# A gated-mix kernel on one core: the down projection of its feed-forward as 2x2 block products in Strassen's form, with GpSimd making sums of blocks

## The chip, the core and the metric

The kernel runs on one core of a Trainium2 chip. The metric is the device time of one execution in microseconds (us). The core's engines are named as the profile names them: PE (TensorE, matmuls), PEld (its weight loads), DVE (VectorE), ACT (ScalarE), POOL (GpSimd) and SP (SyncE, which issues the DMAs). Before the change the median of three runs is 1704.81 us (1704.14 to 1707.67).

## The reference

```python
x = A_x                                             # 1 x 2048 x 576, float32
g = sigmoid((x * gate_w).sum(-1, keepdims=True))    # one gate per token
qkv = x @ wqkv                                      # 32 heads of 18
phi = lambda p: concat([softmax(p), softmax(-p)])   # of q and k after w_phi, per head
kv, z = sum_s phi_k v, sum_s phi_k                  # linear attention
a = (phi_q kv / (phi_q z + 1e-6)) @ wo
gate, up = x @ W_gate, x @ W_up                     # 576 x 4608 each, on the same x = A_x
b = (gate * (gate > 0) * up) @ W_down               # 4608 x 576
out = g * a + (1 - g) * b
```

Every product is float32 by way of two fp32r parts (high and low) of each operand, so that a float32 product is three matmuls: high x high, high x low, low x high.

## The kernel before, in words

The program has two stages. The first (0 to some 415 us) is the attention: projections of 16 tiles of 128 tokens, softmax features, `kv`, and, in four blocks of 512 tokens, the quotient (`sums`, `invert`, `divide`) and the output projection (`project_out`), whose rows go to a DRAM tile `att`. They are scaled by g on the way. POOL works only here (`scale`, L182: one of the two softmax halves of each tile).

The second stage, the feed-forward, runs from some 417 us to the end. Tokens stand along the free dimension. Its outer loop has two halves `hf` of 1024 tokens (two blocks t of 512), its inner loop 36 chunks `c` of 128 hidden rows: 72 units `u`. Gate and up of a chunk, for both token blocks, are a 2x2 block product in Strassen's form (Winograd's variant): seven products `product(ps, u, n, first)` (L720) of seven matmuls of 128x512 each. Their token operands `XO[hf, n]` (tiles `xo`) are made once for each half by `x_operands`: sums of blocks of x on DVE, then high part on ACT, low part on DVE. Their weight operands `wb` and `ws` are made for each chunk from one 768 KB load `wr`: `split_blocks` takes the high and low parts of three blocks (ACT L604, DVE L607, and 32 rows of a third low part, L608), `split_sums` makes four sums of blocks on DVE (L621 to L624, in place) and takes the parts of these. The products accumulate in the PSUM tiles `cx`, `ca`, `cy`; ACT copies three stages of them out (L789, L794, L800), DVE adds the others (L805, L810, L815) and ends with two `scalar_tensor_tensor` that form relu(gate) x up for the two blocks (L822). `split` (L123, L124) takes high and low of each, `hh` and `hl`.

The down projection is a plain product. After every two chunks `down(hf, g)` (L763) adds up the 576 output rows in ten pieces: five row blocks m (four of 128, and one that holds the last 64 rows, high and low) for two token blocks t. A piece takes 6 matmuls, or 4 for the last block: 8 x 6 + 2 x 4 = 56 for two chunks. Two pieces stay in PSUM (`pm`) through the half, eight go through `pd` and are added by DVE to SBUF accumulators `ac` (L770). Its weights come by a load `wdr` and `split_down` (ACT L708, DVE L709, L710). After the last group `finish` multiplies each piece by 1 - g (`ngb`, L740), adds the row block `ga` loaded from `att` (L741) and stores it.

Each engine runs its queue in order. In the feed-forward the order is that in which the tile framework's scheduler puts the instructions of the code; `in_order` pins the code's order on DVE, ACT and SP for the few instructions that `later` traces. The generator `down` is stepped between products, so that the pieces of the group before stand among the products of the present chunks.

## Time and profile before

| what | value |
|---|---|
| median of three runs | 1704.81 us |
| the profiled execution: its time, and its span from the first to the last instruction | 1707.41 us, 1705.6 us |
| PE busy in the span | 97% (7834 matmuls) |
| DVE, ACT, POOL busy in the span | 76%, 37%, 3% |
| mean granted clock of PE | 0.98 |
| bytes read from HBM, written | 108.50 MB, 16.74 MB |

The span is cut into groups by line: a group's row has its instructions' count, the sum of their busy time, the mean of one in ns, and the idle time of the engine just ahead of them with what ended it. Matmuls overlap, so that the 390 ns of one 128x512 matmul is not what it costs; that is read from a stretch in which PE never waits. The window view gives, for stretches of the span, each engine's busy time and count, the clock and the DMA share.

### The profile page before, as it was taken

The numbers are of one execution on the slowest core, as the hardware profiler recorded it, in microseconds if no ns is written. First come the engines' busy times: TensorE is split into PE (matmuls) and PEld (weight loads), VectorE is DVE, ScalarE is ACT, GpSimd is POOL, SyncE is SP. The second block draws the span as 40 slices with busy tenths as digits, with TensorE's granted clock in tenths as the row PEclk, the third lists the DMA queues.
The fourth block names the chain that finished last, engine by engine and source line by source line (L and its number), as shares of the span: only waits on it lengthen the run. The fifth ranks groups of instructions, "written<-read, shape, count | busy, mean of one in ns | idle before, by whom it ended". The sixth has DMA issues, their size and how long they took to land.

```text
span 1705.6 us, 19899 instructions
## 1 busy us (share of the span) xinstructions
PE 1648.6 (97%) x7834; PEld 1379.0 (81%) x7834; DVE 1291.1 (76%) x1966; ACT 624.0 (37%) x895; POOL 46.0 (3%) x53
## 2 busy tenths in 40 slices
PE   9999997988999999999999998999999999999996
PEld 8899995666888888888888886788888888888885
DVE  5877675666778777777778779977777777777776
ACT  4233335554533333333323334433333332333330
POOL 0121210000000000000000000000000000000000
PEclk9899997889999999999999999999999999999998
DMA  5211113535221211122122212421111222121203
GB/s 182 69 37 58 44 44 96 170 127 169 83 70 65 70 51 60 61 65 70 51 70 66 70 51 70 149 83 62 63 61 52 70 65 70 51 70 60 63 18 105
DMA packets 42329, 128.48 MB, mean 75 GB/s; under 512 B 4906, under 2 KB 5546, under 8 KB 42236
## 3 DMA queue, kind: packets, MB, share of 16 engines
q1 hardware_dynamic: 42236, 127.22, 23.1%
q8 instruction: 61, 1.00, 0.2%
q14 instruction: 32, 0.26, 0.0%
HBM read 108.50 MB, written 16.74 MB: 73 GB/s over the span
## 4 chain that ended last, share of the span: by engine, by line
PE 86%; DVE 5%; DMA 4%; ACT 2%; issue 1%; SPq 1%; DVEq 0%; ACTq 0%
PE cx L720 26%; PE pd L763 19%; PE ca L720 13%; PE cy L720 6%; PE pm L763 5%; PE pq L150 4%; PE pk L150 3%; PE pv L150 3%; PE kv L319 2%; PE pwo L150 2%; PE ptr L283 1%; DMA ga<-att 1%; PE po L150 1%; DMA xr<-xs 1%; DMA wdr<-wd 1%
## 5 line engine op out<-in xcount | busy, mean ns | idle before, releaser
L763 PE MATMUL pd<-hh,wd 128*128 128x512 f32 x1008 | 357.5, 390 | 2.2 <-DVE ac L770 2.2
L720 PE MATMUL cx<-xo,ws 128*128 128x512 f32 x1008 | 253.2, 390 | 5.3 <-DVE ws L608 2.2
L720 PE MATMUL cx<-xo,wb 128*128 128x512 f32 x1008 | 252.5, 390 | 2.8 <-DVE o L556 1.4
L720 PE MATMUL ca<-xo,ws 128*128 128x512 f32 x1008 | 253.4, 390 | 0.8 <-DVE ws L608 0.6
L720 PEld LDWEIGHTS cx<-xo,ws 128*128 128x128 f32 x1008 | 188.8, 188 | 46.6 <-ACT g L789 2.7
L763 PE MATMUL pd<-hl,wd 128*128 128x512 f32 x576 | 224.6, 390 | 0.0
L720 PEld LDWEIGHTS cx<-xo,wb 128*128 128x128 f32 x1008 | 188.9, 188 | 43.8 <-DVE o L556 1.9
L763 PEld LDWEIGHTS pd<-hh,wd 128*128 128x128 f32 x1008 | 189.4, 188 | 43.1 <-DVE ac L770 3.5
L720 PEld LDWEIGHTS ca<-xo,ws 128*128 128x128 f32 x1008 | 189.2, 188 | 42.2 <-ACT wd L708 1.0
L770 DVE TENSOR_TENSOR ac<-pd,ac 128x512 f32<-128x512 f32 x272 | 187.5, 690 | 33.1 <-PE pd L763 33.1
L123 ACT ACTIVATE hh<-g 128x512 fp32r<-128x512 f32 x144 | 83.0, 621 | 294.3 <-DVE g L822 294.3
L708 ACT ACTIVATE wd<-wdr 128x576 fp32r<-128x576 f32 x72 | 48.8, 679 | 262.2 <-PE pd L763 256.0
L604 ACT ACTIVATE ws<-wr 128x1536 fp32r<-128x1536 f32 x72 | 107.3, 1490 | 59.5 <-DVE wr L624 59.5
L720 PE MATMUL cy<-xo,wb 128*128 128x512 f32 x504 | 126.6, 389 | 0.0
L763 PEld LDWEIGHTS pd<-hl,wd 128*128 128x128 f32 x576 | 108.4, 188 | 22.4
L607 DVE TENSOR_TENSOR ws<-wr,ws 128x1024 fp32r<-128x1024 f32 x72 | 88.2, 1225 | 44.1 <-ACT ws L604 43.9
L607 DVE TENSOR_TENSOR wb<-wr,wb 128x768 fp32r<-128x768 f32 x72 | 69.0, 958 | 55.1 <-ACT wb L604 53.5
L720 PEld LDWEIGHTS cy<-xo,wb 128*128 128x128 f32 x504 | 94.6, 188 | 19.6
L763 PE MATMUL pm<-hh,wd 128*128 128x512 f32 x288 | 101.0, 389 | 0.0
L800 ACT ACTIVATE g<-cx 128x512 f32<-128x512 f32 x72 | 43.1, 598 | 153.4 <-PE cx L720 147.4
L822 DVE SCALAR_TENSOR_TENSOR g<-g,cx 128x512 f32<-128x512 f32 x72 | 49.5, 687 | 60.2 <-PE cx L720 60.1
L815 DVE TENSOR_TENSOR g<-ca,g 128x512 f32<-128x512 f32 x72 | 49.8, 691 | 58.4 <-PE ca L720 58.3
(180 smaller groups left out, 2555.2 us busy)
## 6 DMA issues: line engine op xcount, KB each, us to landing
wr<-wgu SPq DMA_DIRECT2D x72, 768.0 KB
wdr<-wd SPq DMA_DIRECT2D x72, 288.0 KB
eT<-et SPq DMA_DIRECT2D x12, 594.0 KB
er<-eT SPq DMA_DIRECT2D x12, 594.0 KB
xr<-xs SPq DMA_DIRECT2D x8, 768.0 KB
att<-o SPq DMA_DIRECT2D x16, 256.0 KB
ga<-att SPq DMA_DIRECT2D x16, 256.0 KB
outT<-o SPq DMA_DIRECT2D x16, 256.0 KB
```

What stands on the lines that cost most here:

```text
L123: nc.scalar.activation(hi, src, AF.Copy)
L150: nc.tensor.matmul(ps, w, m, start=i == 0, stop=i == len(pairs) - 1)
L319: nc.tensor.matmul(kv[j // 2][:vn + 1, j % 2, :gn], v[:, j * GS:j * GS + vn + 1], flat(e)[:, c0:c0 + gn], start=False, stop=t == NT - 1, s ...
L604: i = nc.scalar.activation(o[:, :, 0:3], a, AF.Copy)
L607: tt(out=o[:, :, 3:5], in0=a[:, :, 0:2], in1=o[:, :, 0:2].bitcast(F32), op=SUB)
L708: nc.scalar.activation(o[:, :D], w, AF.Copy)
L720: nc.tensor.matmul(ps, w, v, start=first and m == 0, stop=m == len(pairs) - 1, skip_group_check=True)
L763: nc.tensor.matmul(ps, w, v, start=i == 0 and (g == 0 or not perm), stop=i == len(pairs) - 1 and (g == NGR - 1 or not perm))
L770: tt(out=ACC[m, t], in0=ps, in1=ACC[m, t], op=ADD)
L800: nc.scalar.activation(g2, cx, AF.Copy)
L815: tt(out=g2, in0=ca, in1=g2, op=ADD)
L822: nc.vector.scalar_tensor_tensor(out=g, in0=g, scalar=0.0, in1=up, op0=ALU.max, op1=MULT)
```

## The change

1. The down projection becomes seven products too. Two chunks and two token blocks are a 2x2 block of hidden values, and two chunks with two row blocks (rows of `m` and of `2 + m`) are a 2x2 block of weights, for m = 0 and 1. `down(g, s, bank)` has 14 steps s for a pair of chunks, one behind each of the 14 products of the next pair. A step is three matmuls into one of two PSUM tiles, `chain` (products 1, 6, 7, 4, one on top of the other) and `other` (5 with 3, and 2). After each step DVE adds the tile to an accumulator in SBUF (L902). The last 64 rows ride along: two matmuls in four of the seven steps of m = 0, into two PSUM tiles that stay through the half (`REST`, `pm`).
2. The seven hidden operands of a pair are three of its four values and four sums. The sums are made by POOL (L996, L1000, L1082, L1083), and all seven are split into `hh` and `hl` (ACT L932, DVE L938). The weights of a pair come by one load of 576 KB; `down_blocks`, `down_sums_of_blocks` (POOL) and `down_block_sums` make 2 x 7 operands, `rest_weights` those of the 64 rows.
3. POOL also takes over the sums of gate and up weights (L700 to L703) and the 32-row low parts (L681), but for the sums of unit 2.
4. The factor 1 - g is moved: the tokens x of the feed-forward are multiplied by its root. As relu(gate) x up is of degree two in x, the product carries 1 - g. `half_gates` makes the root (ACT's Sqrt), `on_all_rows` spreads it, `scaled_sums` on POOL multiplies the four blocks of x and makes the four sums of blocks, and writes all to a DRAM tile `xt`: for the first half in the attention stage (eight 128x1536 operations), for the second half one 128x768 operation a chunk from chunk 4 on (16 of them). The token operands are loaded from `xt`. For the second half they are made in the two chunks at the change of halves, one step a product (`swap_in`).
5. The accumulators start from `att` (`load_acc`, `load_rest`), so that the end of a half only stores them.
6. The order of all five engines in the feed-forward is that of the code: `chunk(u)` is written as seven slots, each a product, the add of the down step before, and a down step, then the other engines' work, and `in_order` pins it.

PE's queue in the middle of the first half, before (`cx`, `cy` and `ca` are products of gate and up, `pd` a piece of the down projection):

```order
L720 MATMUL cx<-xo,ws 128x512 x7
L720 MATMUL cy<-xo,wb 128x512 x7
L763 MATMUL pd<-hh,wd 128x512
L763 MATMUL pd<-hl,wd 128x512
L763 MATMUL pd<-hh,wd 128x512 x2
L763 MATMUL pd<-hl,wd 128x512
L763 MATMUL pd<-hh,wd 128x512
L720 MATMUL ca<-xo,ws 128x512 x7
```

And now, from the last product of an odd chunk through the first of the even one behind it:

```order
L861 MATMUL cx<-xo,wb 128x512 x7
L887 MATMUL chain<-hh,wd 128x512
L887 MATMUL chain<-hl,wd 128x512
L887 MATMUL chain<-hh,wd 128x512
L861 MATMUL cx<-xo,wb 128x512 x7
L887 MATMUL chain<-hh,wd 128x512
L887 MATMUL chain<-hl,wd 128x512
L887 MATMUL chain<-hh,wd 128x512
L887 MATMUL pm_9283<-hh,w_10329 128x512
L887 MATMUL pm_9283<-hl,w_10329 128x512
```

Three matmuls (five with the 64 rows) now stand behind every product, where six, four or none stood; and at the change of chunks two steps in a row write the tile `chain`, with one product between them.

DVE's queue in the same stage, before, from the last `scalar_tensor_tensor` of a chunk (`g` and `u` are its gate and up values, `wr` the raw weights):

```order
L822 SCALAR_TENSOR_TENSOR g_6780<-g_6780,cx 128x512
L770 TENSOR_TENSOR ac_4098<-pd,ac_4098 128x512
L124 TENSOR_TENSOR hl<-g_6780,hh 128x512
L124 TENSOR_TENSOR hl<-g_6809,hh 128x512
L607 TENSOR_TENSOR wb<-wr,wb 128x3x256
L608 TENSOR_TENSOR wb<-wr,wb 32x3x128
L621 TENSOR_TENSOR wr<-wr 128x384
L622 TENSOR_TENSOR wr<-wr 128x384
```

And now, over the same kind of place, the end of an odd chunk and the start of an even one:

```order
L678 TENSOR_TENSOR ws<-wr,ws 128x4x256
L1066 TENSOR_TENSOR u_9464<-cx,u_9464 128x512
L902 TENSOR_TENSOR ac_9237<-chain,ac_9237 128x512
L835 TENSOR_TENSOR wd<-wdr,wd 128x512
L850 TENSOR_TENSOR w_9480<-wdr,w_9480 128x64
L1078 TENSOR_TENSOR g_9484<-ca,g_9484 128x512
L1079 SCALAR_TENSOR_TENSOR g_9484<-g_9484,u_9464 128x512
L902 TENSOR_TENSOR ac_9260<-other,ac_9260 128x512
L938 TENSOR_TENSOR hl<-g_9484,hh 128x512
L1092 SCALAR_TENSOR_TENSOR g_9439<-g_9439,cx 128x512
L902 TENSOR_TENSOR ac_9318<-chain,ac_9318 128x512
L938 TENSOR_TENSOR hl<-g_9297,hh 128x512
```

The weight sums and 32-row parts have left DVE's queue; an add `ac` now stands between any two steps, and the add of `chain` at the change of chunks stands behind a split, a product and a sum.

POOL's queue in this stage was empty before; from the sum of hidden values (`g`) in an odd chunk through that chunk's last low part it now has (`wdr` are the raw down weights):

```order
L1000 TENSOR_TENSOR g_8649<-g_8700,g_8649 128x512
L681 TENSOR_TENSOR wb<-wr,wb 32x3x128
L700 TENSOR_TENSOR wr<-wr 128x384
L701 TENSOR_TENSOR wr<-wr 128x384
L702 TENSOR_TENSOR wr<-wr 128x384
L703 TENSOR_TENSOR wr<-wr 128x384
L845 TENSOR_TENSOR wdr<-wdr 128x64
L820 TENSOR_TENSOR wdr<-wdr 128x128
L821 TENSOR_TENSOR wdr<-wdr 128x128
L822 TENSOR_TENSOR wdr<-wdr 128x128
L823 TENSOR_TENSOR wdr<-wdr 128x128
L681 TENSOR_TENSOR ws<-wr,ws 32x4x128
```

Sums that DVE made (L621 to L624 before) and the 32-row parts (L608 before) stand here now, with new sums of hidden values and of down weights; eight or nine follow one another without another engine's work between them.

The diff, cut to its core:

```diff
-def in_order(tc, nc):
+def in_order(tc, nc, *engines):
...
+    def scaled_sums(hf, b, sb, c0, n):
...
+        for i, a in enumerate(b):
+            pt(out=a, in0=a, in1=sb[:, i % 2, None, :].to_broadcast([P, 3, n]), op=MULT)
+            yield
+            if i != 1:
+                put((1, 0, 2, 3)[i], a)
+        for i, o, a, c in ((5, b11, b12, b11), (7, b12, b22, b12), (6, b22, b22, b11), (4, b21, b21, b22)):
+            pt(out=o, in0=a, in1=c, op=SUB)
+            yield
+            put(i, o)
...
     for t in range(2, NT - 1):
...
+        if t == 8:
+            half_gates(0)
+            sb = xw.tile([P, 2, TB], F32, name="sb", bufs=1)
...
+            first_half = scaled_sums(0, [xw.tile([P, 3, TB], F32, name="xb") for _ in range(4)], sb, 0, TB)
+        for _ in range(3):
+            next(first_half, None)
...
-            tt(out=a[:, 2], in0=a[:, 2], in1=a[:, 3], op=ADD)
-            tt(out=a[:, 3], in0=a[:, 0], in1=a[:, 3], op=SUB)
-            tt(out=a[:, 0], in0=a[:, 2], in1=a[:, 0], op=SUB)
-            tt(out=a[:, 1], in0=a[:, 1], in1=a[:, 0], op=SUB)
...
+    def low_w_rows(o, a):
+        pt(out=o[64:96, :, 2], in0=a[64:96, :, 2], in1=o[64:96, :, 2].bitcast(F32), op=SUB)
...
+        f = tt if u == 2 else pt
+        f(out=a[:, 2], in0=a[:, 2], in1=a[:, 3], op=ADD)
...
+    hp = ctx.enter_context(tc.tile_pool(name="hp", bufs=8, **CB))
+    pd = ctx.enter_context(tc.tile_pool(name="pd", bufs=1, space=PSUM, **CB))
...
+    def down(g, s, bank):
...
+        mm(ps, o[:, 0, k], h, n in (1, 5, 2), False)
+        mm(ps, o[:, 0, k], l, False, False)
+        mm(ps, o[:, 1, k], h, False, True)
+        if m == 0 and n in (1, 5, 2, 4):
...
+            mm(REST[r], w, h, first and n in (1, 5), False)
+            mm(REST[r], w, l, False, last and n in (2, 4))
...
+            tt(out=a, in0=ps, in1=a, op=ADD)
...
+    def chunk(u):
...
+        def slot(j, ps, n, first):
+
+            product(ps, u, n, first)
+            if PEND:
+                done.extend(PEND.pop()())
+            if q >= 0:
+                PEND.append(down(q, 7 * odd + j, one_bank))
...
+        slot(5, ca, 3, False)
+        flush()
+        if odd:
+            down_block_sums(g, 0, low)
+            rest_weights(g, 3)
...
+        tt(out=g2, in0=ca, in1=g2, op=ADD)
+        nc.vector.scalar_tensor_tensor(out=g2, in0=g2, scalar=0.0, in1=u2, op0=ALU.max, op1=MULT)
+        if odd:
+            high_h(g, 3, g2)
+            pt(out=r[0], in0=g2, in1=r[0], op=SUB)
+            pt(out=r[1], in0=g2, in1=r[1], op=SUB)
...
+        slot(6, cx, 4, False)
...
+        if hf == 0 and c >= 4:
+            next(second, None)
...
+    with in_order(tc, nc, nc.tensor, nc.vector, nc.scalar, nc.gpsimd, nc.sync):
+        for u in range(len(units)):
+            chunk(u)
...
+        put(0, 0, 1)
...
+        add()
+        put(0, 2, 3)
...
+        put(1, 5, 6)
+        add()
+        store_rest(1, 1)
+        store(work)
```

562 lines of the change are left out of this document (391 added, 171 removed).

## The prediction

> **What bounds the kernel now.** I read the windows first: they say which engine has no time left, and where. Columns are the stretch, its length, then busy us (and count) of PE, PEld, DVE, ACT and POOL, the granted clock, DMA share and GB/s.
>
> ```profile
> 100.00:200.00 100.00, 100.00 (x714) 94.48 (x712) 71.79 (x99) 35.77 (x57) 19.95 (x20) 1.00 0.14 48
> 450.00:1030.00 580.00, 580.00 (x2561) 480.41 (x2560) 448.43 (x688) 201.86 (x273) 0.00 (x0) 1.00 0.19 62
> 1030.00:1100.00 70.00, 62.64 (x255) 47.32 (x254) 66.57 (x100) 30.16 (x37) 0.00 (x0) 0.98 0.42 130
> 1110.00:1650.00 540.00, 540.00 (x2383) 447.13 (x2383) 421.61 (x653) 186.81 (x254) 0.00 (x0) 1.00 0.19 61
> 1690.80:1705.60 14.80, 0.00 (x0) 0.00 (x0) 8.42 (x13) 0.63 (x1) 0.00 (x0) 0.61 0.54 154
> ```
>
> In the two stretches of feed-forward PE is busy through all 1120 us, at full clock, and DVE is idle for 250 of them. The chain of waits says the same for the whole span:
>
> ```profile
> PE 86%; DVE 5%; DMA 4%; ACT 2%; issue 1%; SPq 1%; DVEq 0%; ACTq 0%
> ```
>
> So matmuls set the time there. What one costs I take from the distance of the same instruction in two chunks that follow each other (DVE's timeline: start, length, instruction, idle time before):
>
> ```profile
> 703.07 0.69 DVE L822 SCALAR_TENSOR_TENSOR g<-g,cx 128x512 f32<-128x512 f32 x1 [0.90 <-PE cx L720]
> ...
> 714.71 0.69 DVE L805 TENSOR_TENSOR u<-cx,u 128x512 f32<-128x512 f32 x1
> 715.32 0.68 DVE L810 TENSOR_TENSOR g<-cy,g 128x512 f32<-128x512 f32 x1
> ...
> 720.52 0.69 DVE L822 SCALAR_TENSOR_TENSOR g<-g,cx 128x512 f32<-128x512 f32 x1 [0.90 <-PE cx L720]
> ```
>
> A chunk takes 720.52 - 703.07 = 17.45 us. It has 7 x 7 = 49 matmuls of products and half of a group's 56 of the down projection: 77, so 0.2266 us each, and a pair of chunks 34.90 us.
>
> **PE's work.** A pair now has 98 matmuls of products, 14 steps of 3, and 8 for the 64 rows: 148 for 154. Over 36 pairs 216 matmuls go: 216 x 0.2266 = 48.9 us less, and the pair's floor becomes 148 x 0.2266 = 33.54 us. All of it lies on the path, if PE stays as busy as it is.
>
> **DVE's work**, by groups (busy us, mean ns of one, then idle time ahead):
>
> ```profile
> L770 DVE TENSOR_TENSOR ac<-pd,ac 128x512 f32<-128x512 f32 x272 | 187.5, 690 | 33.1 <-PE pd L763 33.1
> L124 DVE TENSOR_TENSOR hl<-g,hh 128x512 fp32r<-128x512 f32 x144 | 92.9, 686 | 1.2 <-ACT hh L123 1.0
> L607 DVE TENSOR_TENSOR ws<-wr,ws 128x1024 fp32r<-128x1024 f32 x72 | 88.2, 1225 | 44.1 <-ACT ws L604 43.9
> L607 DVE TENSOR_TENSOR wb<-wr,wb 128x768 fp32r<-128x768 f32 x72 | 69.0, 958 | 55.1 <-ACT wb L604 53.5
> L608 DVE TENSOR_TENSOR ws<-wr,ws 32x512 fp32r<-32x512 f32 x72 | 49.2, 683 | 1.0
> L621 DVE TENSOR_TENSOR wr<-wr 128x384 f32<-128x384 f32 x72 | 40.2, 558 | 2.3
> L608 DVE TENSOR_TENSOR wb<-wr,wb 32x384 fp32r<-32x384 f32 x72 | 39.6, 550 | 1.0
> L709 DVE TENSOR_TENSOR wd<-wdr,wd 128x512 fp32r<-128x512 f32 x72 | 49.4, 685 | 3.0 <-ACT wd L708 2.9
> L710 DVE TENSOR_TENSOR wd<-wdr,wd 128x64 fp32r<-128x64 f32 x72 | 15.8, 220 | 0.0
> ```
>
> What leaves DVE in a pair is 2 x (4 x 0.558 + 0.550 + 0.683) = 6.93 us of sums and 32-row parts, 8 adds (5.52) and 4 splits of hidden values (2.74), and the down weights' 2 x (0.685 + 0.220) = 1.81: 17.00 us. What comes is 14 adds (9.66), 7 splits (4.80) and weight parts of width 384, 512 (the rows of 0.558 and 0.685, twice) and two narrow ones (0.25 each): 2.99 us. That is 17.45 us, so DVE's load hardly moves: by means a pair cost 28.25 us and now costs 28.70. The windows have DVE busy for 870.04 / 1120 x 34.90 = 27.1 us a pair, 0.96 of the sum of means, since one operation starts before the last one's end (714.71 to 715.32 above is 0.61, not 0.69). So 27.6 us of work for 33.54: 82%, from 78%. By itself it fits.
>
> **POOL beside DVE.** POOL gets 25 operations a pair where it had none. Their price, and what it does to DVE, is in the attention stage, where both scale halves of one tile (min, median, max ns in the first rows; then timelines):
>
> ```profile
> L182 POOL TENSOR_TENSOR e<-e,r x16: 1163/1168/1176, 67.0 to 264.9; 128x576 f32<-128x576 f32 x16
> ...
> L182 DVE TENSOR_TENSOR e<-e,sm x16: 758/760/1492, 41.5 to 246.3; 128x576 f32<-128x576 f32 x16
> ...
> 61.41 1.19 POOL L182 TENSOR_TENSOR e<-e,sm 128x576 f32<-128x576 f32 x1 [15.17 <-DVE sm L244]
> ...
> 61.18 0.69 DVE L174 TENSOR_TENSOR e<-mn,pq 128x576 f32<-128x576 f32 x1
> 61.80 1.42 DVE L182 TENSOR_TENSOR e<-e,sm 128x576 f32<-128x576 f32 x1
> ...
> 81.31 0.76 DVE L182 TENSOR_TENSOR e<-e,sm 128x576 f32<-128x576 f32 x1
> ...
> 81.42 1.69 POOL L182 TENSOR_TENSOR e<-e,sm 128x576 f32<-128x576 f32 x1 [0.51 <-DVE sm L244]
> ...
> L259 POOL MEMSET vt<- 128x6 f32 x16 | 1.7, 108 | 40.3 <-ACT gs L258 21.9 <-ACT vt L255 18.4
> ```
>
> The operation that comes second waits. POOL runs from 61.41 to 62.60; DVE's scale, 0.76 us alone, ends at 63.22, 0.62 behind it, so it began its data some 0.14 us before POOL's end. At 81.31 DVE is first, and POOL takes 1.69 for 1.17. The DVE operation at 61.18, with one input in PSUM, ran 0.46 us into POOL's and took its normal 0.69. So only DVE operations with both inputs in SBUF meet POOL.
>
> POOL's price: 1.168 us less the 0.108 of a tiny memset, over 576 elements, is 1.84 ns an element; an estimate of 1.05, 0.81, 0.34 and 0.23 us for widths 512, 384, 128 and 64. A pair: 8 sums of 384 (6.5), the 32-row parts (3.7), 8 of 128 (2.7), 4 of 512 (4.2), one of 64 (0.2): 17.4 us, 52% of 33.54. DVE has 19 operations with both inputs in SBUF in a pair (7 splits, 4 gate and up parts, 6 down parts, 2 of L1079). At even odds each finds POOL at work with 0.52 and waits for the rest of it, 0.41 us (mean square over twice the mean) less 0.14, rounded up to 0.30: 0.16 each, 3.0 a pair. DVE is then at 30.6 of 33.54.
>
> That still fits on average; it does not at one place. From slot 4 of an odd chunk on, DVE's queue is add, `ws` part, u; add, two down parts, g, L1079; add, split, L1092, and then the add of `chain`, on which PE's step behind the next product waits. Laid against PE, at 0.61 an operation: counted from the end of slot 5's product, the last product ends at 2.27 us (10 matmuls). DVE has g, L1079, add and split to do, 2.44, and comes 0.23 late, since slot 4's 0.96 x (0.69 + 1.225 + 0.69) = 2.50 is more than a slot's 2.27. So L1092 starts at 2.67, the add ends at 2.67 + 0.61 + 0.69 = 3.97, and PE wants the tile at 2.27 + 0.68 + 1.59 = 4.54: 0.57 us to spare, against five meetings of 0.16 = 0.78. That is 0.21 over on the mean; but pairs with few meetings give nothing back, and whether the 0.14 holds when POOL's operations follow one another no row shows. I take 0.5 us a pair; bounds 0 (the fixed order keeps the two apart) and 1.4 (five times the 0.41, less the spare). At the even chunk's end the slots are longer by two matmuls and nothing is left over. 36 x 0.5 = 18 us (0 to 50).
>
> In 16 chunks one 128x768 operation (0.108 + 768 x 0.00184 = 1.52 us) is queued on POOL right at this place: from 0 to 1.38 us each, half of it taken: 16 x 0.75 = 12 us (0 to 22).
>
> Here the Trainium skill, "SBUF — State Buffer", section "Who interferes with whom", gives a rule: the shared pair is locked for a whole instruction and the loser fully blocks. The trace agrees but for the 0.14 us; by the rule without that, a meeting costs 0.21, five cost 0.3 us more than above, and the 18 us would be 29.
>
> **The ends.** At the change of halves 70 us hold 255 matmuls, 57.8 us of work: 12 us lost, while DVE is at 95% with sums of x and the finish. Sums and finish go, but the seven operands (1.22 us each for the wide low part, estimated by the 1225 row) fall on a DVE at 90%; I take half, -5 (-12 to +3). At the end, the last product starts at 1674.31, 60 matmuls follow it, and then PE has nothing to do for 14.80 us:
>
> ```profile
> 1674.31 1.75 PE L720 MATMUL cx<-xo,wb 128*128 128x512 f32 x7
> ...
> 1701.52 0.68 DVE L741 TENSOR_TENSOR o<-o,ga 64x512 f32<-64x512 f32 x1 [0.86 <-DMA ga<-att]
> ```
>
> The span ends 3.4 us behind that last DVE operation, the store. Now the row blocks are there already, and 53 matmuls (12.0), some 3.2 of waits for adds in between, an add (0.69) and the store (3.4) make 19.3 us after the last product's end (1674.31 + 7 x 0.2266 = 1675.9), for 29.7. Less the seven matmuls already counted (1.6) that is -9 (-12 to -4). In the attention eight POOL operations of 1536 (2.9 us each) fall in a stretch where PE never waits (100 to 200 above) and DVE is at 72%. DVE's scale can wait for one of them four times; most is hidden by two tiles of slack: +3 (-2 to +12). The root adds a table load on ACT, at 36% there: nothing, or 1.3 us each if that cover is gone:
>
> ```profile
> L123 ACT ACT_TABLE_LOAD x1 | 1.3, 1283 | 0.7 <-PEq L913 0.7
> ...
> L577 DVE TENSOR_TENSOR xr<-xr,xr 128x1536 f32<-128x1536 f32 x2 | 3.5, 1755 | 0.0
> ```
>
> The middle stage loses four of DVE's sums of x (L577 and its like, 1.755 each, 7.0 us) and gains a second chunk's weight parts (2.2 us); loads from `xt` and `att` stand ahead of weight loads in SP's queue, but DMA's share is 0.42 even where loads bunch (1030 to 1100 above): nothing (-5 to +5).
>
> **Sum.** -48.9 + 18 + 12 - 5 - 9 + 3 = -29.9, rounded to -30. The profiled execution's 1707.4 us (2.6 above the median) becomes 1677.5; against the median 1704.8 that is **1675 us**.
>
> **Rivals.** *All waits hidden.* The order keeps POOL and DVE apart. For it: 18% of DVE's time is free. -48.9 - 5 - 9 + 3: 1645 us. *No change.* PE's waits eat it all: 1.05 us a pair, between my 0.5 and the bound of 1.4, and the 768-wide operations at their bound of 22: -48.9 + 38 + 22 - 11 = 0, 1705 us. For it: DVE at 91% with waits. Against: these need nearly every meeting to fall in the one tight place. The Trainium skill ("Perfetto Trace Analysis", "Optimizing Scalar/DVE Operations") warns so: the two share a read port, and moving work between them might not help. The rows bear out the port, not yet the extent. *Slower: DVE starves behind runs of POOL.* The four sums and four or five small ones are 4 x 0.81 + 4 x 0.34 = 4.6 us in a row in each chunk. If POOL's next operation takes the port ahead of a waiting DVE, the split behind the first add waits 4.6 - 0.61 - 0.14 = 3.8 us, 7.6 a pair, and with 1.5 for the other meetings DVE needs 27.6 + 9.1 = 36.7 us a pair and becomes the bound: 36 x 1.8 - 11 = +54, 1759 us. It decides from 35.2 us a pair (34.9 + 11 / 36). For it: no row has two POOL operations in a row with DVE waiting. Against: each sum reads the one before, and a wait of POOL on itself leaves DVE a gap.
>
> **How the numbers follow.** Forecast 0.50 (1655 to 1697), all hidden 0.20, no change 0.13, starved 0.17. Faster by over 0.2% (3.4 us, about what a measurement tells from no change): 0.50 + 0.20 + 0.04 = 0.74; within: 0.06; slower: 0.17 + 0.03 = 0.20. The range goes to 1640, past the all-hidden case by half of what the ends may give more, and to 1715, past no change; most of the starved case is outside.
>
> **What would show it.** Right: 148 matmuls a pair; PE's waits in the feed-forward on DVE's add into `ac` at even chunks' first step, 0.5 us, more between chunks 5 and 23; DVE `hl`, `wb` and `wd` groups with means above 0.69, 0.96 and 0.62, adds at 0.69; POOL some 52% busy; some 4 us from PE's last matmul to the end, for 14.8. Wrong: PE busy without a break (all hidden), or DVE busy through and PE's waits in every slot (starved), or waits on DMA or ACT, which I priced at nothing.

## The result, and the profile after

The changed kernel takes 1789.28 us (median of four runs, 1787.15 to 1791.25) against 1705.12 for the kernel before (four runs, 1704.14 to 1707.67): a ratio of 1.049, 95% interval 1.0473 to 1.0509. It is 4.9% slower; I had forecast 1675, and the result lies outside my range of 1640 to 1715. The profiled execution has 1788.61 us and a span of 1786.8.

The windows of the kernel after, for stretches that answer to those of before (columns as there: busy us and count of PE, PEld, DVE, ACT and POOL, clock, DMA share, GB/s):

```profile
560.00:840.00 280.00, 256.48 (x1078) 204.69 (x1077) 242.50 (x298) 110.51 (x175) 219.36 (x195) 0.98 0.23 77
1060.00:1160.00 100.00, 76.77 (x291) 59.39 (x290) 75.38 (x93) 41.21 (x63) 70.47 (x59) 0.90 0.36 120
1200.00:1700.00 500.00, 473.36 (x2029) 382.54 (x2029) 431.37 (x565) 210.02 (x333) 364.94 (x342) 0.99 0.17 61
```

Before the change PE was busy through all of the feed-forward's steady stretches; now it waits there, and the count of matmuls says how much. A pair of chunks has 148: 148 x 500 / 2029 = 36.5 us a pair in the second half, 148 x 280 / 1078 = 38.4 in the stretch with the 768-wide POOL operations, where 34.90 stood before and 33.54 is PE's floor. POOL is busy for 73% and 78%. The chain of waits for the whole span, which had PE at 86% before, now goes round between DVE, PE and POOL:

```profile
DVE 28%; PE 27%; POOL 25%; ACT 11%; issue 5%; DMA 3%; SPq 2%; POOLq 0%; ACTq 0%; DVEq 0%
```

The last `scalar_tensor_tensor` of a chunk cuts the time into stages. DVE's timeline after, at chunks 0, 6, 34, 39 and 71, then the same of before:

```profile
428.00 0.69 DVE L1092 SCALAR_TENSOR_TENSOR g<-g,cx 128x512 f32<-128x512 f32 x1
539.03 0.67 DVE L1092 SCALAR_TENSOR_TENSOR g<-g,cx 128x512 f32<-128x512 f32 x1
1066.09 0.68 DVE L1092 SCALAR_TENSOR_TENSOR g<-g,cx 128x512 f32<-128x512 f32 x1
1184.95 0.67 DVE L1092 SCALAR_TENSOR_TENSOR g<-g,cx 128x512 f32<-128x512 f32 x1
1766.95 0.68 DVE L1092 SCALAR_TENSOR_TENSOR g<-g,cx 128x512 f32<-128x512 f32 x1
```

```profile
432.17 0.69 DVE L822 SCALAR_TENSOR_TENSOR g<-g,cx 128x512 f32<-128x512 f32 x1
528.54 0.69 DVE L822 SCALAR_TENSOR_TENSOR g<-g,cx 128x512 f32<-128x512 f32 x1 [0.90 <-PE cx L720]
1017.23 0.69 DVE L822 SCALAR_TENSOR_TENSOR g<-g,cx 128x512 f32<-128x512 f32 x1 [0.90 <-PE cx L720]
1117.59 0.69 DVE L822 SCALAR_TENSOR_TENSOR g<-g,cx 128x512 f32<-128x512 f32 x1 [0.53 <-PE cx L720]
1676.09 0.69 DVE L822 SCALAR_TENSOR_TENSOR g<-g,cx 128x512 f32<-128x512 f32 x1 [0.86 <-PE cx L720]
```

| stage | before, us | after, us | difference |
|---|---|---|---|
| to the end of chunk 0 | 432.2 | 428.0 | -4.2 |
| chunks 1 to 6 | 96.4 | 111.0 | +14.7 |
| 7 to 34 | 488.7 | 527.1 | +38.4 |
| 35 to 39, the change of halves | 100.4 | 118.9 | +18.5 |
| 40 to 71 | 558.5 | 582.0 | +23.5 |
| to the end of the span | 29.5 | 19.9 | -9.7 |

Together +81.2 us, the difference of the two spans. The rows also show that DVE waited for PE at this place before (`<-PE cx` at its side) and no longer does.

DVE's groups after, and what ended DVE's idle time ahead of them:

```profile
L938 DVE TENSOR_TENSOR hl<-g,hh 128x512 fp32r<-128x512 f32 x252 | 234.9, 943 | 7.5 <-ACT hh L932 1.4
L902 DVE TENSOR_TENSOR ac<-chain,ac 128x512 f32<-128x512 f32 x284 | 193.3, 681 | 16.7 <-PE chain L887 16.6
L678 DVE TENSOR_TENSOR wb<-wr,wb 128x768 fp32r<-128x768 f32 x72 | 99.7, 1384 | 21.9 <-ACT wb L675 21.8
L678 DVE TENSOR_TENSOR ws<-wr,ws 128x1024 fp32r<-128x1024 f32 x72 | 91.5, 1271 | 101.8 <-ACT ws L675 101.8
L835 DVE TENSOR_TENSOR wd<-wdr,wd 128x512 fp32r<-128x512 f32 x72 | 79.3, 1102 | 1.5 <-ACT wd L832 1.5
L835 DVE TENSOR_TENSOR wd<-wdr,wd 128x384 fp32r<-128x384 f32 x72 | 75.3, 1046 | 6.9 <-ACT wd L832 6.9
L844 DVE TENSOR_TENSOR w<-wdr,w 128x128 fp32r<-128x128 f32 x36 | 37.1, 1031 | 0.0
```

The add, with one input in PSUM, keeps its 0.68 us. The operations that read two SBUF tiles are longer, by the means: the split 0.94 for 0.69, `wb` 1.38 for 0.96, the down parts 1.10 and 1.05, the narrow part (128x128) 1.03; `ws` hardly, 1.27 for 1.22. And 101.8 us of idle time stand ahead of the `ws` part, for 44.1 before. Its cause is in the list of waits, two steps back:

```profile
ACT ws L675 <- POOL wr L703: 213.7, 70, 6.6
ACT wd L832 <- POOL wdr L823: 126.8, 72, 5.5
DVE ws L678 <- ACT ws L675: 101.8, 67, 4.6
PE chain L887 <- DVE ac L902: 80.1, 46, 3.3
```

DVE's two longest waits of the second half alone (1200 to 1700 us):

```profile
DVE ws L678 <- ACT ws L675: 37.1, 27, 1.8
DVE g L1053 <- PE cy L861: 15.1, 17, 0.9
```

POOL's price (min, median, max ns of an operation; the forms of L299 differ):

```profile
L1082 POOL TENSOR_TENSOR g<-g,g x36: 1279/1288/1299, 443.9 to 1765.2; 128x512 f32<-128x512 f32 x36
L703 POOL TENSOR_TENSOR wr<-wr x71: 991/1014/1859, 382.6 to 1741.4; 128x384 f32<-128x384 f32 x71
L823 POOL TENSOR_TENSOR wdr<-wdr x72: 455/1327/1532, 439.9 to 1773.9; 128x128 f32<-128x128 f32 x72
L299 POOL TENSOR_TENSOR xb<-xb x12: 1835/2172/3882, 150.0 to 844.1; 128x768 f32<-128x768 f32 x8, 128x1536 f32<-128x1536 f32 x4
```

By the shortest of each, which I take as undisturbed, it is 1.28, 0.99, 0.455 and 1.835 us for widths 512, 384, 128 and 768; I had 1.05, 0.81, 0.34 and 1.52. L823 comes just when DVE runs its `ws` part, and takes 1.33 in the median for 0.455.

The forecast place is there. The end of an odd chunk and the start of the next, PE's timeline, then DVE's, then POOL's:

```profile
1437.50 1.75 PE L861 MATMUL cx<-xo,wb 128*128 128x512 f32 x7
1441.38 0.50 PE L887 MATMUL chain<-hh,wd 128*128 128x512 f32 x1 [2.13 <-DVE ac L902]
```

```profile
1433.13 1.31 DVE L678 TENSOR_TENSOR ws<-wr,ws 128x1024 fp32r<-128x1024 f32 x1 [1.80 <-ACT ws L675]
...
1438.85 1.28 DVE L938 TENSOR_TENSOR hl<-g,hh 128x512 fp32r<-128x512 f32 x1
1440.05 0.67 DVE L1092 SCALAR_TENSOR_TENSOR g<-g,cx 128x512 f32<-128x512 f32 x1
1440.64 0.68 DVE L902 TENSOR_TENSOR ac<-chain,ac 128x512 f32<-128x512 f32 x1
```

```profile
1438.29 1.29 POOL L1082 TENSOR_TENSOR g<-g,g 128x512 f32<-128x512 f32 x1 [2.16 <-DVE g L1079]
1439.53 1.72 POOL L1083 TENSOR_TENSOR g<-g,g 128x512 f32<-128x512 f32 x1
```

The split at 1438.85 ends 0.55 behind POOL's end at 1439.58; POOL's next operation takes 1.72 in its turn. PE waits 2.13 us, where I had 0.5.

### The profile page after: what moved, and what is told of

Same layout as the page of the kernel before. It is cut to its first block, busy times and chain, and to the rows that moved or that the text cites. A ratio compares the mean times of both kernels' runs of the same rounds, so it can differ in the third digit from the quotient of the medians.

```text
span 1786.8 us, 20994 instructions
## 1 busy us (share of the span) xinstructions
PE 1644.5 (92%) x7618; PEld 1349.7 (76%) x7618; DVE 1446.3 (81%) x1911; ACT 742.0 (42%) x1178; POOL 1085.1 (61%) x984
## 4 chain that ended last, share of the span: by engine, by line
DVE 28%; PE 27%; POOL 25%; ACT 11%; issue 5%; DMA 3%; SPq 2%; POOLq 0%; ACTq 0%; DVEq 0%
POOL wb L681 5%; ACT ws L675 5%; DVE ac L902 4%; POOL wr L700 4%; POOL wr L701 4%; DVE ws L678 4%; DVE hl L938 4%; PE cx L861 4%; DVE wd L835 3%; POOL wr L703 3%; POOL wr L702 3%; PE pq L152 3%; PE pk L152 3%; PE ca L861 3%; DVE g L1079 3%
## 5 line engine op out<-in xcount | busy, mean ns | idle before, releaser
L887 PE MATMUL chain<-hh,wd 128*128 128x512 f32 x568 | 230.1, 405 | 80.2 <-DVE ac L902 80.1
L932 ACT ACTIVATE hh<-g 128x512 fp32r<-128x512 f32 x252 | 158.3, 629 | 319.1 <-DVE g L1092 174.1
L938 DVE TENSOR_TENSOR hl<-g,hh 128x512 fp32r<-128x512 f32 x252 | 234.9, 943 | 7.5 <-ACT hh L932 1.4
L902 DVE TENSOR_TENSOR ac<-chain,ac 128x512 f32<-128x512 f32 x284 | 193.3, 681 | 16.7 <-PE chain L887 16.6
L887 PEld LDWEIGHTS chain<-hh,wd 128*128 128x128 f32 x568 | 107.7, 190 | 123.2 <-DVE ac L902 101.3
L675 ACT ACTIVATE ws<-wr 128x1536 fp32r<-128x1536 f32 x72 | 107.3, 1490 | 214.9 <-POOL wr L703 213.7
L681 POOL TENSOR_TENSOR wb<-wr,wb 32x384 fp32r<-32x384 f32 x72 | 107.0, 1486 | 117.8 <-DMA dn<-R 106.3
L678 DVE TENSOR_TENSOR ws<-wr,ws 128x1024 fp32r<-128x1024 f32 x72 | 91.5, 1271 | 101.8 <-ACT ws L675 101.8
L887 PE MATMUL other<-hh,wd 128*128 128x512 f32 x426 | 166.9, 392 | 1.5 <-DVE ac L902 1.5
L835 DVE TENSOR_TENSOR wd<-wdr,wd 128x384 fp32r<-128x384 f32 (+1 forms) x144 | 154.7, 1074 | 8.4 <-ACT wd L832 8.4
L1000 POOL TENSOR_TENSOR g<-g,g 128x512 f32<-128x512 f32 x36 | 46.5, 1291 | 181.6 <-DVE hl L938 153.9
L902 DVE TENSOR_TENSOR ac<-other,ac 128x512 f32<-128x512 f32 x213 | 145.6, 684 | 4.3 <-PE other L887 4.2
L832 ACT ACTIVATE wd<-wdr 128x384 fp32r<-128x384 f32 (+1 forms) x144 | 82.6, 574 | 134.7 <-POOL wdr L823 126.8
L678 DVE TENSOR_TENSOR wb<-wr,wb 128x768 fp32r<-128x768 f32 x72 | 99.7, 1384 | 21.9 <-ACT wb L675 21.8
```

The lines of the kernel that those rows point to most:

```text
L675: nc.scalar.activation(o[:, :, 0:3], a, AF.Copy)
L678: tt(out=o[:, :, 3:5], in0=a[:, :, 0:2], in1=o[:, :, 0:2].bitcast(F32), op=SUB)
L681: pt(out=o[64:96, :, 2], in0=a[64:96, :, 2], in1=o[64:96, :, 2].bitcast(F32), op=SUB)
L832: nc.scalar.activation(o[:, 0], a, AF.Copy)
L835: tt(out=o[:, 1], in0=a, in1=o[:, 0].bitcast(F32), op=SUB)
L887: mm = lambda ps, w, v, a, z: nc.tensor.matmul(ps, w, v, start=a, stop=z, skip_group_check=True)
```

## The experiments

Four theories. **A, a loop**: DVE's `wb` part, POOL's four sums, ACT's and DVE's `ws` part and the rest of DVE's queue follow one another from chunk to chunk; that loop sets the pair, and PE's wait is what is left over. **B, a late add** (my prediction): only the add of `chain` is late, by what DVE waits behind POOL. After the first four runs came **D, the port**: DVE's operations with two SBUF inputs and POOL's reads shut each other out, and that alone holds PE back; and its rival **F**: DVE's own work is too much, with or without POOL. Kernels ran once each, but for before and after (four runs in the result above), best2 and best3 (four) and best4 (eight). The end of chunk 0 lies between 423 and 432 us in runs whose attention is the same, so a few us between two single runs say nothing. The second column is the time; the others are the mean pair, in us, between chunks 6 and 22 (with the 768-wide operations), 24 and 34, and 40 and 70, and the time from chunk 34 to 39, read as in the table above. PE's floor is 33.54.

| kernel | us | 6-22 | 24-34 | 40-70 | 34 to 39 |
|---|---|---|---|---|---|
| before | 1705.1 | 34.9 | 34.9 | 34.9 | 100.4 |
| after | 1789.3 | 38.5 | 36.5 | 36.5 | 118.9 |
| alt_banks | 1783.0 | 38.4 | 36.3 | 36.3 | 117.5 |
| sums_aside | 1791.8 | 38.5 | 36.5 | 36.5 | 118.3 |
| memsets | 1652.9 | 33.55 | 33.55 | 33.55 | 103.5 |
| wb_first | 1823.4 | 39.3 | 37.5 | 37.5 | 122.0 |
| alt_down | 1831.8 | 39.5 | 38.0 | 37.9 | 120.5 |
| alt_hidden | 1753.4 | 37.8 | 35.5 | 35.5 | 114.7 |
| alt_both | 1805.0 | 38.0 | 37.2 | 37.2 | 122.9 |
| no_768 | 1774.1 | 36.5 | 36.5 | 36.5 | 119.7 |
| stored | 1742.1 | 38.5 | 36.5 | 33.95 | 100.8 |
| moved | 1811.3 | 36.4 | 36.4 | 36.5 | 119.4 |
| best | 1734.2 | 35.5 | 35.5 | 33.55 | 99.8 |
| best2 | 1738.0 | 35.5 | 35.5 | 33.55 | 100.1 |
| fill_sums | 1741.0 | 37.5 | 35.2 | 35.2 | 112.4 |
| fill_rest | 1665.0 | 33.55 | 33.55 | 33.55 | 108.6 |
| best3 | 1730.4 | 35.5 | 35.5 | 33.55 | 100.4 |
| best4 | 1714.5 | 37.8 | 35.5 | 33.55 | 99.8 |

### More time for the add: alt_banks

```diff
-        key = "chain" if n == 1 else "other"
+        key = "chain" if (n == 1) == (m == 0) else "other"
```

> The PSUM tiles of the down steps swap roles in the second row block (m = 1), so that no two steps in a row write the same tile at a change of chunks; the add has one more slot (about 2.3 us) there. Theory A (a loop: DVE's wb part, POOL's four sums, ACT's and DVE's ws part, the rest of DVE's queue, the next wb part; it sets the period by itself and PE's wait is only what is left over): nothing gained, 1775 to 1792 us, 36.3 us a pair in the second half as now. Theory B (only the add of chain is late, by DVE's waits for the port behind POOL): the 2.1 us wait of each pair goes, 36 x 2.1 = 75 less, 1710 to 1735 us, about 34 us a pair.

1783.0 us, 36.3 us a pair: B falls. The wait of the down step nearly goes, from 80.1 to 11.1 us, and turns up at another place, where PE waits for DVE to read a product (the list of waits of alt_banks; the first was 7.0 us in after):

```profile
PE cx L861 <- DVE u L1066: 60.5, 66, 1.3
PE chain L887 <- DVE ac L902: 11.1, 12, 1.9
```

The wait that the trace names on PE is a symptom: DVE is late everywhere, and PE waits wherever it needs DVE next. What DVE itself waits for is nearly always the same: of its 70.8 us of idle time from 1200 to 1700 us, 62.0 stand ahead of the `ws` part, which needs ACT and, behind ACT, the last of POOL's sums.

### Nobody waits for the sums: sums_aside

From chunk 3 on the four sums go to one scratch tile:

```diff
-        f(out=a[:, 2], in0=a[:, 2], in1=a[:, 3], op=ADD)
...
+        s = wraw.tile([P, 1, 3, P], F32, name="aside", bufs=1)
+        for o, i, j, op in ((2, 2, 3, ADD), (3, 0, 3, SUB), (0, 2, 0, SUB), (1, 1, 0, SUB)):
+            pt(out=s[:, o % 1], in0=a[:, i], in1=a[:, j], op=op)
```

> POOL's four sums of gate and up weights are made as before, at the same price and with the same use of the port, but into a scratch tile that nobody reads (from chunk 3 on the ws parts take the raw blocks, so these sums are left out of the result). Theory A: the loop is open, the 1.7 to 1.8 us that DVE idles ahead of each ws part go, and a pair comes to 33.6 to 34.8 us: 1700 to 1740 us. Theory B: DVE meets POOL as often as before and the add of chain stays late: 1770 to 1790 us.

1791.8 us, no change to be told from one run: A falls in the form that I gave it. ACT and DVE no longer wait for the sums of gate and up, but the down sums stand behind them in POOL's queue, and ACT waits for those now, 333.5 us for 126.8:

```profile
ACT wd L834 <- POOL wdr L825: 333.5, 72, 6.7
```

So a later result of the same run took the first one's place. The chain that ended last still passes through POOL, for 33% of the span. That all of POOL's results were set free at once, with POOL's reads left in place, was not tried; so a loop through POOL, ACT and DVE is not excluded by this run, only the one through these four sums.

### POOL without reads: memsets

```diff
-    pt = nc.gpsimd.tensor_tensor
+    def pt(out, in0, in1, op):
...
+        for _ in range(k):
+            nc.gpsimd.memset(out, 0.5)
+        if e:
+            nc.gpsimd.memset((out if len(out.shape) == 2 else out[:, 0])[:, :e], 0.5)
```

> Every POOL operation of the feed-forward becomes two memsets of its output plus a short one, about as long together (1.3 us for 128x512, 1.05 for 128x384, 0.5 for 128x128), in the same place of the order; POOL then reads nothing from SBUF (its sums and low parts are left out of the result). If the price lies in DVE's waits for the port: DVE's hl, wb, ws and wd parts fall to 0.69, 0.96, 1.23 and 0.6 to 0.7 us, 5.5 us a pair less on DVE, and the time to 1690 to 1715 us. If it lies in POOL's slowness alone (its sums are late whoever waits for the port): 1765 to 1790 us. Theories A and B both allow the first; A with half of the 5.5 us in the loop would give some 34 us a pair.

1652.9 us, 37 below what I expected at best: PE is at its floor in all the steady stages, also between chunks 6 and 22. The second half's window, DVE's groups and POOL's memsets:

```profile
1200.00:1600.00 400.00, 400.00 (x1767) 331.37 (x1766) 320.30 (x489) 181.40 (x285) 235.30 (x789) 1.00 0.18 64
```

```profile
L955 DVE TENSOR_TENSOR hl<-g,hh 128x512 fp32r<-128x512 f32 x252 | 170.1, 687 | 10.1 <-ACT hh L949 2.1
L695 DVE TENSOR_TENSOR ws<-wr,ws 128x1024 fp32r<-128x1024 f32 x72 | 87.9, 1221 | 6.6 <-ACT ws L692 5.7
L695 DVE TENSOR_TENSOR wb<-wr,wb 128x768 fp32r<-128x768 f32 x72 | 69.0, 958 | 24.9 <-ACT wb L692 24.8
L861 DVE TENSOR_TENSOR w<-wdr,w 128x128 fp32r<-128x128 f32 x36 | 10.2, 284 | 0.0
```

```profile
L687 POOL MEMSET wr<- 128x384 f32 x568 | 238.2, 420 | 129.5 <-DMA wr<-wgu 109.1 <-DVE wb L695 0.2 <-POOL wb L689 0.2
```

POOL is busy for 59% of the time, and what it writes is waited for as before. Its own waits for inputs that it does not overwrite are gone, and some stand-ins are a little short: that of a sum of weights lasts two of 0.42 and one of 0.15 us, 0.99 for 0.99, that of a sum of hidden values 1.21 for 1.28. But DVE's parts are back at 0.687, 0.958 and 0.284 us, and the idle time ahead of `ws` is 6.6 us for 101.8. So POOL at its undisturbed pace costs PE nothing in the steady stages; with its reads go 1788.6 - 1652.9 = 136 us. By which way they cost it, DVE's longer operations or POOL's own longer ones that bring its results late, this run does not tell: both go at once. The Trainium skill ("SBUF — State Buffer", "Who interferes with whom") says that a DVE operation with two SBUF inputs contends with a GpSimd operation that reads SBUF and not with one that only writes it; this trace agrees, at 0.687 us beside memsets and 0.943 beside sums.

### Another order: wb_first

```diff
+        blocks(v, high_w)
+        blocks(v, low_w)
+        blocks(v, low_w_rows)
         if not odd:
             if q >= 0:
                 high_h(q, 6, R[0]); low_h(q, 6, R[0])
...
```

> In slot 0 the wb parts (ACT, DVE and POOL's 32 rows) go ahead of the splits of hidden values, and POOL's sum of hidden values goes behind the four sums of weights; its split moves to slot 4. Nothing is left out. Theory A: the loop is shorter by one or two hl operations, 0.9 to 2.4 us a chunk: 34.0 to 35.0 us a pair, 1710 to 1745 us. Theory B: the add of chain stands where it stood, 1780 to 1795 us.

1823.4 us, slower than either theory had it, and no test of the loop: ACT's `wb` part now stands ahead of the high parts of hidden values and waits for PE's last product, and DVE's splits wait for ACT, 146.9 us where it was 1.4:

```profile
DVE hl L938 <- ACT hh L932: 146.9, 70, 4.8
```

### From POOL to DVE: alt_down, alt_hidden, alt_both

The first change is in alt_down and alt_both, the second in alt_hidden and alt_both:

```diff
     def down_sums_of_blocks(g, m):
...
-        pt(out=a[:, 2], in0=a[:, 2], in1=a[:, 3], op=ADD)
+        tt(out=a[:, 2], in0=a[:, 2], in1=a[:, 3], op=ADD)
...
-                pt(out=R[2], in0=R[2], in1=R[0], op=SUB)
+                tt(out=R[2], in0=R[2], in1=R[0], op=SUB)
```

> The alternating PSUM tiles of alt_banks, and the sums of down weights (eight of 128x128 and one of 128x64 a pair) go from POOL to DVE; nothing is left out. Theory D (DVE's operations with two SBUF inputs and POOL's exclude each other, and a pair is 36.3 us because these two sums together fill it: some 24 us of POOL and 12 to 13 of DVE): POOL gives up 8 x 0.53 + 0.35 = 4.6 us, DVE takes 8 x 0.2 + 0.1 = 1.7: 2.9 us a pair less, 33.5 to 34.5 us, 1695 to 1725 us in all. Theory F (DVE has no time left; its own load sets the pair): 1.7 us a pair more, 1830 to 1845 us.

> The alternating PSUM tiles, and the four 128x512 sums of hidden values of a pair go from POOL to DVE; nothing is left out. Theory D: POOL gives up 4 x 1.36 = 5.4 us of the shared time and its waits for DVE at these places, DVE takes 4 x 0.61 = 2.4: 3.0 us a pair less, 33.5 to 34.5 us, 1690 to 1725 us. Theory F: 2.4 us a pair more, 1850 to 1870 us.

> Both moves of alt_down and alt_hidden at once: DVE's work without waits rises to some 31.7 us a pair, POOL keeps 14 us. Theory D: 36.3 - 2.9 - 3.0 is below PE's floor of 33.54, so PE or DVE with what is left of its waits sets it: 33.6 to 35 us a pair, 1675 to 1725 us. Theory F: 4.1 us a pair more, over 1900 us.

Against alt_banks, the four wide sums on DVE take off 0.8 us a pair (1753.4 us): less than D's 3.0, and F, which had 2.4 more, falls with it. The nine narrow ones add 1.6 (1831.8 us): D as a sum of times fails there, and F has the number but not the reason. Both moves at once come to 37.2 us a pair (1805.0 us), which neither theory had. The reason for the narrow ones is in the timelines of alt_down, DVE's four sums of 128x128 and three of POOL's beside them:

```profile
1440.77 1.10 DVE L820 TENSOR_TENSOR wdr<-wdr 128x128 f32<-128x128 f32 x1
1441.91 1.06 DVE L821 TENSOR_TENSOR wdr<-wdr 128x128 f32<-128x128 f32 x1
1443.01 1.04 DVE L822 TENSOR_TENSOR wdr<-wdr 128x128 f32<-128x128 f32 x1
1444.08 0.29 DVE L823 TENSOR_TENSOR wdr<-wdr 128x128 f32<-128x128 f32 x1
```

```profile
1440.38 1.35 POOL L701 TENSOR_TENSOR wr<-wr 128x384 f32<-128x384 f32 x1
1441.81 1.02 POOL L702 TENSOR_TENSOR wr<-wr 128x384 f32<-128x384 f32 x1
1442.90 0.99 POOL L703 TENSOR_TENSOR wr<-wr 128x384 f32<-128x384 f32 x1
```

The two take turns. Each of the first three DVE operations ends 0.14 to 0.16 us behind one of POOL's, so one that takes 0.29 alone takes 1.0 to 1.1 beside a run of POOL. What such a move costs DVE here is not the operation's own length but about one POOL operation each, so short ones that fall into a run are dear. In alt_hidden only one of the four wide sums meets POOL: L996 takes 1.31 us on DVE, the other three 0.69. In the second half of alt_down and of alt_both DVE is busy for 97% and 99%, so that there it is the bound by its busy time alone:

```profile
1200.00:1700.00 500.00, 461.73 (x1956) 370.49 (x1955) 485.74 (x662) 196.60 (x316) 274.38 (x210) 0.98 0.16 58
1200.00:1700.00 500.00, 471.02 (x1993) 368.83 (x1993) 493.13 (x725) 201.78 (x322) 193.94 (x162) 1.00 0.17 60
```

### Which of POOL's operations: no_768, fill_sums, fill_rest

The first change is that of no_768; the second that of fill_sums, with `fill` the memsets of above. fill_rest has them in all other places of the feed-forward:

```diff
-            pt(out=a, in0=a, in1=sb[:, i % 2, None, :].to_broadcast([P, 3, n]), op=MULT)
+            if not hf:
+                pt(out=a, in0=a, in1=sb[:, i % 2, None, :].to_broadcast([P, 3, n]), op=MULT)
...
-        f = tt if u == 2 else pt
+        f = tt if u == 2 else fill
```

> The change as it is, without the sixteen 128x768 POOL operations that scale the second half's tokens in chunks 4 to 23 (the second half's tokens then are neither scaled nor summed). Theory D: each held the port for its 1.83 us and 2.5 us a pair were lost in these chunks: 22 to 30 us less, 1758 to 1767 us, and 36.3 us a pair there as elsewhere. Theory F: they are not on DVE; what they cost is only where one stands ahead of a sum that DVE or ACT waits for, 0 to 12 us less.

> Only the four gate and up sums of a chunk (from chunk 3 on) become memsets of about their length, as in memsets; POOL's other operations stay and read SBUF. The sums are left out of the result. If the loss follows the time that POOL reads SBUF (8.7 of some 24 us a pair go): a pair loses some 1.2 to 1.8 us for 2.8, 34.7 to 35.4 us, 1725 to 1755 us. If it is the run of sums that ACT and DVE wait for: under 34 us a pair, 1670 to 1700 us.

> The converse: the gate and up sums stay, and all other POOL operations of the feed-forward become memsets of about their length (their results are left out). If the loss follows the time that POOL reads: 8.7 of 24 us stay and DVE's waits fall below the slack of 6 us a pair: 33.6 to 34.3 us, 1655 to 1690 us. If it is the run of sums: 35.3 us a pair or more, over 1740 us.

Without the 768-wide operations the pair is 36.5 us in all stages. They cost 1788.6 - 1774.1 = 14.5 us by the whole times, and 18.7 in chunks 5 to 24, where they stand (383.4 us in after for 364.7; the end of chunk 0, which they do not touch, is 3.5 us later in no_768): less than D's 22 and more than F's 12. With the sums of gate and up as memsets (8 x 0.99 of some 22 us of POOL's operations a pair) the loss over the floor falls from 2.9 to 1.7 us a pair; with those sums alone reading SBUF it is nothing, and DVE's split is at 0.724 us. So the four sums alone are not to blame. fill_rest, fill_sums and after have some 8, 14 and 22 us of operations that read, and lose 0, 1.7 and 2.9 us a pair, and both fills came as expected if the loss follows the time that POOL reads. That it sets in where DVE's slack is used up is my reading of these three points. The amount alone does not give the loss: alt_hidden and alt_down both leave POOL some 17 us, with more work on DVE, and lose 1.95 and 4.4.

### Without the contention in one half: stored

```diff
-        f(WB[u], RAW[u][:, 0:3])
+        if u < NC:
+            f(WB[u], RAW[u][:, 0:3])
+        else:
+            nc.sync.dma_start(WB[u].bitcast(F32), wbd[:, units[u][1]])
...
```

> The change as it is, but the first half also writes its finished gate and up operands (wb and ws, 2.24 MB a chunk) to DRAM, and the second half loads them in place of the raw weights: from chunk 36 on there are no four sums and no low parts of gate and up weights on POOL, and no wb and ws parts on DVE and ACT. Nothing is left out of the result. Theory D (POOL's and DVE's reads of SBUF exclude each other, and that alone holds PE back): the second half goes to PE's floor, 33.5 to 33.9 us a pair, and the first stays at 36.3 and 38.4 us: 1725 to 1750 us. If the order of the down steps with one tile for chain held PE back by itself, the second half would stay over 35 us a pair: over 1765 us.

1742.1 us. The first half stays as it was but for its start, and the second comes to within 0.4 us a pair of the floor, with every instruction of PE in its old order and one tile for `chain`. Two windows of stored:

```profile
560.00:840.00 280.00, 254.83 (x1071) 202.68 (x1071) 243.67 (x299) 112.29 (x178) 218.80 (x195) 0.98 0.54 200
1300.00:1600.00 300.00, 299.10 (x1310) 244.76 (x1309) 217.41 (x328) 90.31 (x177) 87.72 (x116) 1.00 0.40 150
```

This takes work from DVE as well as reads from POOL, so it does not tell D from F, as memsets does; it shows that the order and the one tile for `chain` hold PE up by 0.4 us a pair at most. The change of halves comes back to 100.8 us, and in memsets, with all of DVE's work, to 103.5: of its extra 18.5 some 15 go with POOL's reads. DMA at a share of 0.40 to 0.54 does not hold PE up in these stretches. At the start the new stores do cost time: chunks 1 to 4 take 83.8 us for 72.1 in after, and ACT waits 13.2 us there for a load of raw weights.

### Toward a faster kernel: moved, best, best2, best3, best4

```diff
+    for _ in second_half():
+        pass
...
-            keep_operands(0)
-            keep_operands(1)
+        if u == 1:
+            keep_operands(1)
```

The first change is that of moved, which puts the 768-wide operations into the attention; best is alternating tiles, alt_hidden's move, stored and moved together. In best2 and best3 they are stepped through two blocks of the attention. The second change, shown against best2, is in best3 and best4: the stores of the first two chunks are spread. best4 is best3 with the 768-wide operations back in chunks 4 to 23.

> The change as it is, but the sixteen 128x768 POOL operations for the second half's tokens stand in the attention's last 100 us, where POOL is idle, in place of chunks 4 to 23; the first half's token operands start one block later for it. Nothing is left out. Theory D: chunks 4 to 23 go from 38.4 to 36.4 us a pair as without these operations, 14 to 20 us less, and the attention gives 0 to 10 of it back: 1768 to 1785 us.

> Alternating PSUM tiles, sums of hidden values on DVE, stored operands for the second half, and the 768-wide operations in the attention, all at once; nothing is left out. By the sum of the parts: 1753 of alt_hidden, 16 pairs x 1.95 less in the second half, 15 less for chunks 4 to 23, 5 to 10 less at the change of halves: 1690 to 1715 us, 35.5 us a pair in the first half, 33.6 in the second.

> As best, but the 768-wide operations and their DMAs are spread over the first two blocks of the attention's last stage, two steps at a place, so that SyncE's queue does not hold the attention's own loads behind them (24.9 us in best). If that was what made best late, the feed-forward starts some 40 us earlier, with 35.5 and 33.6 us a pair as in best: 1688 to 1702 us, 0 to 1% below the kernel before. If POOL's use of the port or the DMA rate in the attention was it: 1715 to 1735 us.

> As best2, but the stores of the first two chunks' operands (4.5 MB at once at the start of chunk 0) are spread over chunks 0 and 1, so that the loads of the first token operands do not stand behind them (21.8 us in best2). If that made best2's start late: 1698 to 1715 us; the operations in the attention cost 10 to 12 us there. If not: 1730 to 1740 us.

> As best3, but with the 768-wide operations back in chunks 4 to 23: 428 us at the first chunk's end as in the change, 37.8 us a pair in chunks 6 to 22, 35.5 to chunk 34, 33.6 in the second half: 1700 to 1715 us, within 0.5% of the kernel before.

The pairs came as expected; the move into the attention did not, so moved, best and best2 are slower than forecast and best3 lies in the range for the case that the stores were not the cause. Chunk 0 ends at 469 to 478 us in these four, for 428. In best ACT waits 26.9 us (5.9 in after) for the attention's own loads `er`, which SyncE issues behind the new stores; in best2 that is 6.8, but chunk 0 ends no earlier, with 21.8 us of waits for the first token operands, and spreading the stores in best3 moved it only to 471. In these four PE is busy for 30 to 34 of the 60 us from 300 to 360, for 55 in after. What holds it up there besides the loads was not settled.

best4, without the move, is the fastest that leaves nothing out: 1714.5 us, ratio to before 1.0052 (1.0035 to 1.0070). It regains 75 of the 84 us and does not beat the kernel before (best2 1.0196, 1.0174 to 1.0219; best3 1.0140, 1.0116 to 1.0163). Its first half, at 37.8 and 35.5 us a pair, is over the 34.9 of before.

## Why the prediction was wrong, point by point

**PE's work**: 7618 matmuls for 7834, the 216 less. Right, and worth what I said: memsets, with all of the change but POOL's reads, takes 1652.9 us, 54.5 under the execution before, against -48.9 - 11 = -60 in my sum without waits.

**The step that failed** is "POOL beside DVE", with its two sentences "DVE is then at 30.6 of 33.54. That still fits on average; it does not at one place." It counted DVE's work and its waits for the port, and left out DVE's waits for what ACT makes of POOL's results, which I priced at nothing. In the second half of after DVE is busy for 431.37 / 500 x 36.5 = 31.5 us of a pair, which would still fit into 33.54. But of its 5.0 idle us, 37.1 / 13.7 = 2.7 stand ahead of `ws` and 0.4 ahead of `wb`, both on ACT (the window holds 13.7 pairs; in memsets the whole run has 6.6 us ahead of `ws`): 34.6 together, more than PE's floor. Most of the rest are waits for PE, 1.7, so that PE and DVE hold each other up.

The port itself costs more than I had. DVE's work alone is 320.30 / 400 x 33.55 = 26.9 us, as memsets shows it (I had 27.6). Waits behind POOL, by the means of after less those of memsets, are 7 x 0.256 for the splits, 2 x 0.426 for `wb`, 2 x 0.050 for `ws`, 2 x (0.420 + 0.496) for the down parts (0.682 and 0.550 us in memsets), 0.747 for the narrow part and 2 x 0.104 for L1079 (0.796 for 0.692): 5.5 us where I had 3.0. So DVE's queue, with its waits for the port and for what ACT makes of POOL's sums, is longer than PE's work, and PE follows it. How the loss divides between the two kinds of wait stays open, since no run took away one and left the other. Three things were wrong in the step.

1. *POOL's price.* I took 1.84 ns an element from an operation whose second input is a broadcast row. With two full inputs it is (1835 - 455) / (768 - 128) = 2.16 ns, and 0.18 us for each operation: 22 us a pair and not 17.4. A page would have helped: the Trainium skill ("GPSIMD Engine Reference", "Elementwise — side-by-side cycle accounting") has 4497 ns for 2048 elements, by division an estimate of 2.2 ns each, and the rows here agree with 2.16.
2. *Even odds.* I let 19 operations meet POOL by chance. In a run of POOL's operations DVE comes out of one wait into the next, one POOL operation for each of its own (shown in alt_down), and POOL waits in its turn (L823, 0.455 us undisturbed, has a median of 1.327).
3. *The wait for POOL's results.* I priced waits on ACT at nothing. ACT waits 213.7 us for the last sum, and DVE's queue stands behind ACT's part.

So the term of 18 us (0 to 50) was some 36 x 2.9 = 105 us, and its bound was of no use, as it allowed for one late add and not for a late queue. The rival that came nearest is the one I gave 0.17, DVE starved behind POOL, and the time is 30 us past its 1759: DVE's queue does hold PE back. But it does so at 31.5 us of busy time a pair, not at the 36.7 of that rival, and not by waiting for a whole run; DVE gets its turn after each operation of POOL's, pays with each, and then waits for POOL's results by way of ACT.

**The 768-wide operations**: 12 us forecast, 14.5 to 18.7 measured. **The end**: -9 forecast, -9.7. **The attention**: +3 forecast, -4.2 to the end of chunk 0, within what this differs by from run to run. **The change of halves**: -5 forecast, +18.5; by memsets 15.4 of it (118.9 - 103.5) are the same contention, which I had not applied there though the chunks at the change have all of POOL's operations too. Even without it, memsets has 3.1 us more than before where I had less; that is not explained. I also had no term for the start: chunks 1 to 4 take 72.1 us in after and 64.2 in memsets, for 61.5 before.

**The signs** that I named for being right were there in kind: 148 matmuls a pair, PE's waits on the add at the even chunk's first step, longer DVE parts, adds at 0.68, 4.8 us from PE's last matmul (1782.0) to the end. In kind, each of these fits a kernel of 1675 us and one of 1789; only their sizes spoke against me, 2.1 us of PE's wait for 0.5 and POOL 73% busy for 52%. One of my signs of being wrong was there too, and told the two apart: a wait on ACT, the idle time ahead of `ws`.

## What to carry to other kernels

Where GpSimd works beside VectorE, count GpSimd's operations that read SBUF and VectorE's that read two SBUF tiles: in these traces each that fell into a run of the other engine paid up to a whole operation of it, short ones as much as long ones. And ask who waits for GpSimd's results, which come late by the same meetings. Averages of busy time (82% and 52% in my forecast, 86% and 73% in the trace) don't show that, and the wait on PE only shows where PE needed DVE next; an experiment that swaps the reads for writes of equal length, or removes the work from half of the loop, does. Moving work off DVE paid here only where POOL read little: 8 us of a pair cost PE nothing, 14 did.

## What the runs showed of the hardware

- Beside POOL's memsets DVE's operations keep the time that they have with POOL idle (0.687 us for the split, 0.958 for `wb`; 0.686 and 0.958 before); beside POOL's sums a 0.29 us operation took 1.04 to 1.10.
- POOL's price goes by the elements of a row, not by the rows: a 32x512 low part (L681) took 1.28 us as the 128x512 sum did.
- Stores of 2240 KB a chunk in the first half of stored (200 GB/s, DMA share 0.54) left the steady pairs at 38.5 and 36.5 us, as without them; chunks 1 to 4 took 11.7 us longer.
